# Decode block with cached attention: keys turned by VectorE block transposes, column-tiled row matmuls, and one ring for the whole load stream

## The chip, the cores and the metric

The kernel runs on one core of a Trainium2 chip. The metric is the device time of one execution in microseconds (us); where several runs exist, their median is quoted.

The time of a run is about 2 us longer than the span in its profile, which goes from the first to the last instruction (before: 455.95 against 453.9). Positions inside the profile are counted from the start of the span.

## The reference

One decode step for a batch of 8: an adaLN block around grouped-query attention with a cache, then an adaLN block around a gated MLP. Everything is bf16.

```python
# x [8,1,1024], c [8,1024], w_mod [1024,6144], wq [1024,4096], wo [4096,1024]
# k_cache, v_cache [8,4,8192,128]   (32 query heads share 4 key/value heads)
# W_gate, W_up [1024,3584], W_down [3584,1024]
mod = silu(c) @ w_mod            # six rows: sa, ca, ga, sb, cb, gb
h = layernorm(x) * (1 + ca) + sa
q = h @ wq                       # [8,32,128]
p = softmax(q @ k^T / sqrt(128)) # over 8192 keys
x = x + ga * ((p @ v) @ wo)
h = layernorm(x) * (1 + cb) + sb
x = x + gb * ((relu(h @ W_gate) * (h @ W_up)) @ W_down)
```

The caches are 134 MB and the weights 51 MB; every byte is used once. A "head" below is one pair of batch and key/value head: 32 of them, each with 2 MB of K and 2 MB of V.

## The kernel before

The kernel is written engine by engine. SP issues the weight and K loads, ACT issues the V loads. Weights have four slots of 2 MB, K has four, V three; each load waits for the last reader of its slot.

```python
NW = 4
NV = 3
NKT = 4
# ... (cut)
def issue_k(eng, n):
    b, p = n // G, n % G
    slot = n % NKT
    if n - NKT >= 0:
        eng.wait("pe", ("sdone", n - NKT))
    eng.dma(T.ksl[:, slot, :], A_k_cache[b, p].rearrange("(k c) d -> k (c d)", k=128), "k%d" % slot)

def issue_v(eng, n):                       # called on ACT's queue
    # ... (cut)
    if n - NV >= 0:
        eng.wait("pe", ("pvdone", n - NV))
    eng.dma(T.vsl[:, slot, :], A_v_cache[b, p].rearrange("(k c) d -> k (c d)", k=128), "v%d" % slot)
```

Scores and the value product both take a block of the cache as the stationary operand (of a matmul's two operands the one that a weight load brings in first; the other is called the moving one), so that each head needs 64 matmuls of eight columns for each. Softmax is done once for a whole batch element (four heads), with the keys in the partitions.

```python
# scores of one head: 64 matmuls, K block stationary
for cix in range(NCX):
    pe.op(lambda e, ...: e.matmul(
        T.S_ps[:, col:col + REP], kv[:, cix, :], T.qT[:, b, REP * p:REP * (p + 1)], start=True, stop=True), ...)
# ... (cut)
# the order on PE
for b in range(B):
    st_phase(b)
    if b >= 1:
        pv_pairs(b - 1, [0, 1])
    softmax_pe_1(b)
    if b >= 1:
        pv_pairs(b - 1, [2, 3])
    softmax_pe_2(b)
```

All projections take the weights as stationary blocks of 128 x 128 with an eight-column moving operand. W_down is loaded in rows of 2 KB, W_gate and W_up in rows of 7 KB:

```python
wblocks.append(("gu", kc, [(lambda r: r[:, 0:F], B_W_gate[128 * kc:128 * (kc + 1), :]),
                           (lambda r: r[:, 4096:4096 + F], B_W_up[128 * kc:128 * (kc + 1), :])]))
# ... (cut)
B_W_down[r0:r0 + rr, :].rearrange("(kk p) n -> p kk n", p=128)
# ... (cut: after the last W_down matmul)
dve.op(... tT <- tT * gb); dve.op(... outT_b <- tT + x1T)
# eight transposes on PE, one copy on DVE, one store on SP
```

Of the kernel before, what the change touches and what calls it, by code (L numbers as in the profile page):

```python
# [11 lines left out]
class _Eng:  # L12

    def __init__(self, K, name):
        self.K = K
        self.name = name
        self.count = 0
        self.e = None
        self.sem = None
        self.muted = True  # L20

    def _live(self):
        return self.K.emit and not self.muted

    def op(self, fn, key=None, sync=True):
        if sync:
            self.count += 1
        if self._live():
            ins = fn(self.e)
            if sync:  # L30
                ins.then_inc(self.sem, 1)
        if key is not None:
            self.mark(key)
        return self.count

    def mark(self, key):
        k = (self.name, key)
        if self.K.emit:
            assert self.K.ev[k] == self.count, (k, self.K.ev[k], self.count)
        else:  # L40
            assert k not in self.K.ev, k
            self.K.ev[k] = self.count

    def wait(self, eng_name, key):
        if self._live():
            val = self.K.ev[(eng_name, key)]
            self.e.wait_ge(self.K.engs[eng_name].sem, val)

    def wait_self(self):
        if self._live() and self.count > 0:  # L50
            self.e.wait_ge(self.sem, self.count)

    def wait_dma(self, sem_name, value):
        if self._live():
            self.e.wait_ge(self.K.dsem[sem_name], value)

    def dma(self, out_ap, in_ap, sem_name):
        c = self.K.dcnt.get(sem_name, 0) + 16
        self.K.dcnt[sem_name] = c
        if self._live():  # L60
            self.e.dma_start(out_ap, in_ap).then_inc(self.K.dsem[sem_name], 16)  # L61
        return c


class _K:
    pass


class _T:
    pass  # L70


DBG = {}


def bass_adaLN_cond__gqa_block_cached__glu_gated_reglu__decode_kernel(
    nc: bass.Bass,
    A_x: bass.AP,
    A_k_cache: bass.AP,
    A_v_cache: bass.AP,  # L80
    A_wq: bass.AP,
    A_wo: bass.AP,
    B_x: bass.AP,
    B_W_gate: bass.AP,
    B_W_up: bass.AP,
    B_W_down: bass.AP,
    c: bass.AP,
    w_mod: bass.AP,
    out: bass.AP,
):  # L90
    B, _, D = A_x.shape
    _, G, Sk, Dh = A_k_cache.shape
    HQD = A_wq.shape[1]
    Hq = HQD // Dh
    REP = Hq // G
    F = B_W_gate.shape[1]
    assert B == 8 and D == 1024 and Dh == 128 and Hq == 32 and G == 4 and REP == 8
    assert F % 128 == 0 and w_mod.shape[1] == 6 * D
    assert Sk % 128 == 0
    NCX = Sk // 128  # L100
    NCOL = NCX * G * REP
    assert NCOL <= 2048
    KC = D // 128
    NKC2 = F // 128
    inv_sqrt_dh = float(Dh) ** -0.5
    EPS = 1e-5
    NW = 4
    NV = 3
    NKT = 4

    K = _K()
    K.ev = {}
    K.emit = False
    K.dcnt = {}
    K.pe_rank = None
    K.engs = {nm: _Eng(K, nm) for nm in ("sp", "act", "pool", "dve", "pe")}

    wblocks = []
    for kc in range(KC):
        wblocks.append(("mod", kc, [(lambda r: r[:, 0:6 * D], w_mod[128 * kc:128 * (kc + 1), :])]))  # L120
    for jb in range(KC // 2):
        wblocks.append(("wq", jb, [(lambda r: r[:, 0:2 * HQD].rearrange("p (k n) -> p k n", n=HQD),
                                    A_wq[256 * jb:256 * (jb + 1), :].rearrange("(kc p) n -> p kc n", p=128))]))
    for blk in range(4):
        wblocks.append(("wo", blk, [(lambda r: r[:, 0:KC * 1024].rearrange("p (k n) -> p k n", n=1024),
                                     A_wo[1024 * blk:1024 * (blk + 1), :].rearrange("(hh d) n -> d hh n", d=128))]))
    for kc in range(KC):
        wblocks.append(("gu", kc, [(lambda r: r[:, 0:F], B_W_gate[128 * kc:128 * (kc + 1), :]),
                                   (lambda r: r[:, 4096:4096 + F], B_W_up[128 * kc:128 * (kc + 1), :])]))
    wd_rows = []  # L130
    r0 = 0
    while r0 < F:
        rr = min(1024, F - r0)
        wd_rows.append((r0, rr))
        r0 += rr
    for di, (r0, rr) in enumerate(wd_rows):
        wblocks.append(("wd", di, [(lambda r, rr=rr: r[:, 0:(rr // 128) * 1024].rearrange("p (k n) -> p k n", n=1024),
                                    B_W_down[r0:r0 + rr, :].rearrange("(kk p) n -> p kk n", p=128))]))
    assert F <= 4096 and 6 * D <= 8192
    widx = {(w[0], w[1]): i for i, w in enumerate(wblocks)}  # L140
    n_phaseA = widx[("wo", 0)]

    last_k_user = {}
    for n in range(B * G):
        last_k_user[n % NKT] = n
    last_v_user = {}
    for n in range(B * G):
        last_v_user[n % NV] = n
    big_regions = Sk >= KC * 1024
    regionsC = [("w", j) for j in range(NW)]  # L150
    if big_regions:
        regionsC += [("k", j) for j in range(NKT)] + [("v", j) for j in range(NV)] + [("s", 0)]
    blocksC = list(range(n_phaseA, len(wblocks)))
    load_order = list(blocksC)
    wplan = {}
    _cnt = {}
    region_last = {}
    for i in range(n_phaseA):
        region = ("w", i % NW)
        free = ("pe", ("wdone", region_last[region])) if region in region_last else None  # L160
        semname = "w%d" % (i % NW)
        _cnt[semname] = _cnt.get(semname, 0) + 16 * len(wblocks[i][2])
        wplan[i] = (region, free, semname, _cnt[semname])
        region_last[region] = i
    holder_t = {}
    for r in regionsC:
        holder_t[r] = region_last[r] if r in region_last else (n_phaseA - 0.5)
    assign = {}
    for i in load_order:
        r = min(regionsC, key=lambda rr_: (holder_t[rr_], regionsC.index(rr_)))  # L170
        assign[i] = r
        holder_t[r] = i
    _wj = [0]
    for i in load_order:
        region = assign[i]
        if region in region_last and region_last[region] >= n_phaseA:
            free = ("pe", ("wdone", region_last[region]))
        elif region[0] == "w":
            free = ("pe", ("sdone", min(B * G - 1, (2 + _wj[0]) * G + G - 1)))
            _wj[0] += 1  # L180
        elif region[0] == "k":
            free = ("pe", ("pvdone", (B - 2) * G + G - 1))
        elif region[0] == "v":
            free = ("pe", ("pvdone", last_v_user[region[1]]))
        else:
            free = ("pe", ("pvdone", B * G - 1))
        semname = {"w": "w%d", "k": "ck%d", "v": "cv%d", "s": "cs%d"}[region[0]] % region[1]
        _cnt[semname] = _cnt.get(semname, 0) + 16 * len(wblocks[i][2])
        wplan[i] = (region, free, semname, _cnt[semname])
        region_last[region] = i  # L190

    T = _T()

    def run():
        K.dcnt = {}
        for e in K.engs.values():
            e.count = 0
        sp, act, pool, dve, pe = (K.engs[n] for n in ("sp", "act", "pool", "dve", "pe"))

        def wregion(i):  # L200
            region = wplan[i][0]
            if region[0] == "s":
                return T.scr[:, 0:8192]
            base = {"w": T.wslot, "k": T.ksl, "v": T.vsl}[region[0]]
            return base[:, region[1], 0:8192]

        def load_wblock(eng, i):
            kind, idx, pieces = wblocks[i]
            region, free, semname, val = wplan[i]
            if free is not None:  # L210
                eng.wait(free[0], free[1])
            r = wregion(i)
            v = None
            for dst_fn, src in pieces:
                v = eng.dma(dst_fn(r), src, semname)
            assert v == val, (i, v, val)

        def pe_wait_wblock(i):
            pe.wait_dma(wplan[i][2], wplan[i][3])

        PB = [T.X_ps, T.OT_ps]

        def issue_k(eng, n):
            b, p = n // G, n % G
            slot = n % NKT
            if n - NKT >= 0:
                eng.wait("pe", ("sdone", n - NKT))
            eng.dma(T.ksl[:, slot, :], A_k_cache[b, p].rearrange("(k c) d -> k (c d)", k=128), "k%d" % slot)

        def issue_v(eng, n):  # L230
            b, p = n // G, n % G
            slot = n % NV
            if n - NV >= 0:
                eng.wait("pe", ("pvdone", n - NV))
# [537 lines left out]
```

## Time and profile before

| | before |
|---|---|
| time, median of 3 runs | 455.95 us (455.82 to 457.14) |
| span of the profile | 453.9 us |
| moved by DMA | 186.40 MB, mean 411 GB/s |
| busy: PE, DVE | 40%, 22% |
| mean granted TensorE clock | 0.96 of full speed |

The first lines to look at are those of the page's 40 slices: the mean busy share of the 16 DMA engines, in tenths, and what they moved.

```profile
DMA  7999999999999999999999999999999989999992
GB/s 309 431 431 426 422 435 428 429 430 372 427 429 424 435 422 425 422 433 422 430 423 430 431 416 430 430 428 419 436 424 432 394 357 428 420 423 424 414 405 77
```

DMA is at 9 (90% or more) in nearly every slice. PE and DVE have room. This kernel is bound by its loads, and a gain has to show in this row. The next view of the page lists the DMA queues: packets, bytes, and the share of the time of 16 engines that they took.

```profile
q1 hardware_dynamic: 17008, 118.54, 62.5%
q10 hardware_dynamic: 4608, 67.11, 34.8%
q8 instruction: 45, 0.74, 0.6%
```

q1 carries SP's loads, q10 ACT's. q8 carries instructions that PE fetches: 45 packets of 16 KB. They take 0.6% of the engines' time.

The third view is a table of windows. The columns are the window, its width, busy time of PE, weight loads, DVE, ACT and POOL with the number of instructions, the granted clock, the DMA share and GB/s.

```profile
core 0: us, PE busy (x) PEld busy (x) DVE busy (x) ACT busy (x) POOL busy (x), PEclk, DMA share, GB/s
0.00:12.00 12.00, 2.36 (x78) 2.25 (x79) 5.87 (x12) 3.79 (x4) 1.28 (x9) 1.00 0.81 317
44.00:52.00 8.00, 3.18 (x104) 3.00 (x104) 1.71 (x6) 0.00 (x0) 0.00 (x0) 1.00 1.00 422
100.00:118.00 18.00, 12.10 (x390) 11.24 (x390) 5.44 (x4) 0.00 (x0) 0.00 (x0) 1.00 0.96 392
350.00:370.00 20.00, 12.26 (x390) 11.43 (x390) 2.99 (x4) 0.00 (x0) 0.00 (x0) 1.00 0.90 369
440.00:454.00 14.00, 7.45 (x232) 6.93 (x232) 2.47 (x9) 0.00 (x0) 0.00 (x0) 0.50 0.36 136
```

The full rate is about 428 GB/s: 425 to 430 in long undisturbed stretches. With that as the yardstick (an estimate), a window's lost time is its width times (1 - rate / 428). That is 3.1 us at the start, 1.5 us in the dip near 110 us, 2.8 us in the dip near 360 us and 9.5 us at the end.

The start and the end can be read closer. The first lines are from the timeline (start, duration, engine, line, operation, count); the second set is the end of the chain of work that ended last.

```profile
0.74 0.39 SPq L61 DMA_DIRECT2D stage_b<-in_c_dram  x1
1.51 8.36 SPq L61 DMA_DIRECT2D wslot<-in_w_mod_dram  x5
8.09 1.42 PE L569 MATMUL X_ps<-siluT,wslot 128*128 128x8 bf16 x48 [2.63 <-DMA wslot<-in_w_mod_dram]
```

```profile
447.29 1.34 PE X_ps L651 x45
448.63 0.87 PE OT_ps L651 x32
450.32 1.03 PE PT_ps L660 x8
451.37 0.68 DVE stage_b L482
```

The first weight load is issued at 1.51 us, behind two small loads. The last piece of W_down is used from 447.29 us, and 6.6 us pass from there to the end. The groups of instructions give the price of one instruction (busy us, mean ns, then the idle time before them with what ended it):

```profile
L525 PE MATMUL OT_ps<-scr,vsl 128*128 128x8 bf16 x2048 | 60.1, 168 | 87.5 <-DMA vsl<-in_A_v_cache_dram 76.7
L508 PE MATMUL S_ps<-qT,ksl 128*128 128x8 bf16 x2048 | 58.3, 168 | 89.5 <-DMA ksl<-in_A_k_cache_dram 76.5
L427 DVE TENSOR_REDUCE guacc<-scr 128x32 f32<-128x2048 bf16 x8 | 28.5, 3568 | 15.8 <-ACT scr L324 15.8
```

### The profile page before, as it was taken

To read this page: it belongs to the slowest core of one execution; us is meant where nothing else is said; L and a number is where in the kernel's file an instruction comes from. 1 tells how busy PE (TensorE), PEld (TensorE's weight loads), DVE (VectorE), ACT (ScalarE), POOL (GpSimd) and SP (SyncE) were. 2 spreads that over 40 slices of the span, in tenths; PEclk is the share of its full clock that TensorE was granted. 3 is DMA by queue.
4 is the path that set the end of the run, shared out by engine and by line. 5 is a ranking of instruction groups with operands and counts; after the bars stand their busy time and mean duration, and the time that the engine had idled before them with its cause. 6 is when DMAs were issued, how large, how long until landed. Compare 5 with 4: busy or idle time off the path is not lost.

```text
span 453.9 us, 11940 instructions
## 1 busy us (share of the span) xinstructions
PE 183.6 (40%) x5784; PEld 170.6 (38%) x5784; DVE 100.9 (22%) x120; ACT 22.5 (5%) x16; POOL 1.3 (0%) x9
## 2 busy tenths in 40 slices
PE   1212433418445226072407240733073573364655
PEld 1212433307345226062406240633063462263655
DVE  5000200062322320043004300430043043003321
ACT  3000001010100100001000100100010011000000
POOL 1000000000000000000000000000000000000000
PEclk9999999999999999999999999999999999999555
DMA  7999999999999999999999999999999989999992
GB/s 309 431 431 426 422 435 428 429 430 372 427 429 424 435 422 425 422 433 422 430 423 430 431 416 430 430 428 419 436 424 432 394 357 428 420 423 424 414 405 77
DMA packets 21662, 186.40 MB, mean 411 GB/s; under 512 B 1624, under 2 KB 1624, under 8 KB 11376
## 3 DMA queue, kind: packets, MB, share of 16 engines
q1 hardware_dynamic: 17008, 118.54, 62.5%
q10 hardware_dynamic: 4608, 67.11, 34.8%
q8 instruction: 45, 0.74, 0.6%
q14 instruction: 1, 0.01, 0.0%
HBM read 185.63 MB, written 0.02 MB: 409 GB/s over the span
## 4 chain that ended last, share of the span: by engine, by line
DMA 65%; PE 19%; DVE 6%; issue 5%; another core or an unknown queue 3%; ACT 1%; SPq 1%
DMA ksl<-in_A_k_cache_dram 43%; DMA vsl<-in_A_v_cache_dram 12%; DMA wslot<-in_w_mod_dram 10%; PE S_ps L508 7%; PE OT_ps L525 4%; PE X_ps L612 2%; DVE guacc L427 2%; PE X_ps L634 1%; PE OT_ps L634 1%; DVE scr L422 1%; PE X_ps L651 1%; ACT scr L324 1%; PE S_ps L494 1%; SPq L61 1%
## 5 line engine op out<-in xcount | busy, mean ns | idle before, releaser
L525 PE MATMUL OT_ps<-scr,vsl 128*128 128x8 bf16 x2048 | 60.1, 168 | 87.5 <-DMA vsl<-in_A_v_cache_dram 76.7
L508 PE MATMUL S_ps<-qT,ksl 128*128 128x8 bf16 x2048 | 58.3, 168 | 89.5 <-DMA ksl<-in_A_k_cache_dram 76.5
L525 PEld LDWEIGHTS OT_ps<-scr,vsl 128*128 128x128 bf16 x2048 | 57.3, 104 | 89.8 <-DMA vsl<-in_A_v_cache_dram 77.8
L508 PEld LDWEIGHTS S_ps<-qT,ksl 128*128 128x128 bf16 x2048 | 56.5, 104 | 91.2 <-DMA ksl<-in_A_k_cache_dram 74.1
L410 DVE TENSOR_REDUCE guacc<-S_ps 128x32 f32<-128x2048 f32 x8 | 18.3, 2292 | 145.5 <-PE S_ps L508 145.5
L427 DVE TENSOR_REDUCE guacc<-scr 128x32 f32<-128x2048 bf16 x8 | 28.5, 3568 | 15.8 <-ACT scr L324 15.8
L324 ACT ACTIVATE scr<-scr 128x2048 bf16<-128x2048 f32 x8 | 15.3, 1909 | 286.4 <-DVE scr L422 286.4
L422 DVE TENSOR_TENSOR scr<-S_ps,guacc 128x2048 f32<-128x2048 f32 x8 | 18.3, 2291 | 0.3
L569 PE MATMUL X_ps<-siluT,wslot 128*128 128x8 bf16 x192 | 5.8, 168 | 17.4 <-DMA wslot<-in_w_mod_dram 17.4
L569 PE MATMUL OT_ps<-siluT,wslot 128*128 128x8 bf16 x192 | 5.8, 168 | 16.5 <-DMA wslot<-in_w_mod_dram 16.5
L569 PEld LDWEIGHTS X_ps<-siluT,wslot 128*128 128x128 bf16 x192 | 5.4, 104 | 17.7 <-DMA wslot<-in_w_mod_dram 15.0
L569 PEld LDWEIGHTS OT_ps<-siluT,wslot 128*128 128x128 bf16 x192 | 5.4, 104 | 16.8 <-DMA wslot<-in_w_mod_dram 16.8
L430 DVE RECIPROCAL guacc<-X_ps 1x32 f32<-1x32 f32 x8 | 2.8, 346 | 37.5 <-PE X_ps L542 37.5
L612 PE MATMUL X_ps<-ot_sb,wslot 128*128 128x8 bf16 x256 | 7.3, 168 | 4.2 <-issue 3.5
L612 PEld LDWEIGHTS X_ps<-ot_sb,wslot 128*128 128x128 bf16 x256 | 7.1, 104 | 4.4 <-issue 3.6
L413 DVE TENSOR_REDUCE guacc<-X_ps 32x1 f32<-32x128 f32 x8 | 2.2, 278 | 22.9 <-PE X_ps L534 22.9
L537 PEld LDWEIGHTS X_ps<-guacc,ones 32*128 32x128 f32 x16 | 4.0, 306 | 8.7 <-DVE guacc L415 8.7
L537 PE MATMUL X_ps<-guacc,ones 32*128 32x32 f32 x16 | 5.0, 406 | 5.1 <-DVE guacc L415 5.1
L386 DVE TENSOR_TENSOR modT<-OT_ps,modT 128x384 f32<-128x384 f32 x4 | 2.2, 558 | 19.5 <-PE OT_ps L569 19.5
L545 PE MATMUL X_ps<-guacc,ones 1*128 1x32 f32 x16 | 5.0, 406 | 3.5 <-DVE guacc L430 3.5
L587 PE MATMUL X_ps<-hT,wslot 128*128 128x8 bf16 x128 | 3.7, 168 | 6.2 <-DMA wslot<-in_A_wq_dram 6.2
L587 PE MATMUL OT_ps<-hT,wslot 128*128 128x8 bf16 x128 | 3.7, 168 | 6.0 <-DMA wslot<-in_A_wq_dram 6.0
(88 smaller groups left out, 107.3 us busy)
## 6 DMA issues: line engine op xcount, KB each, us to landing
vsl<-in_A_v_cache_dram ACTq DMA_DIRECT2D x32, 2048.0 KB, 18.7
ksl<-in_A_k_cache_dram SPq DMA_DIRECT2D x32, 2048.0 KB, 29.4
wslot<-in_w_mod_dram SPq DMA_DIRECT2D x8, 1536.0 KB, 22.5
wslot<-in_A_wq_dram SPq DMA_DIRECT2D x4, 2048.0 KB, 17.0
wslot<-in_A_wo_dram SPq DMA_DIRECT2D x4, 2048.0 KB, 38.5
wslot<-in_B_W_down_dram SPq DMA_DIRECT2D x3, 2048.0 KB, 20.3
ksl<-in_B_W_gate_dram SPq DMA_DIRECT2D x4, 896.0 KB, 23.8
ksl<-in_B_W_up_dram SPq DMA_DIRECT2D x4, 896.0 KB, 25.5
```

The lines of the kernel that those rows point to most:

```text
L324: act.op(lambda e: e.activation(T.pt[:, b % 2, 0:NCOL], T.ssub[:, 0:NCOL], ACT.Exp), key=("exp", b))
L410: dve.op(lambda e: e.tensor_reduce(T.mpart[:, :], T.S_ps[:, 0:NCOL].rearrange("p (c j) -> p j c", c=NCX), AX.X, ALU.max), key=("mpart", b))
L422: dve.op(lambda e: e.tensor_tensor(out=T.ssub[:, 0:NCOL].rearrange("p (c j) -> p c j", c=NCX), in0=T.S_ps[:, 0:NCOL].rearrange("p (c j) -> ...
L427: dve.op(lambda e, b=b: e.tensor_reduce(T.lpart[:, :], T.pt[:, b % 2, 0:NCOL].rearrange("p (c j) -> p j c", c=NCX), AX.X, ALU.add), key=(" ...
L508: pe.op(lambda e, b=b, p=p, kv=kv, cix=cix, col=col: e.matmul(T.S_ps[:, col:col + REP], kv[:, cix, :], T.qT[:, b, REP * p:REP * (p + 1)], ...
L525: pe.op(lambda e, p=p, cix=cix, col=col, vv=vv, ptv=ptv: e.matmul(T.OT_ps[:, col:col + REP], vv[:, cix, :], ptv[:, cix, REP * p:REP * (p + ...
L537: pe.op(lambda e: e.matmul(T.X_ps[:, 128:160], T.ones[0:32, 0:128], T.diag[0:32, 0:32], start=True, stop=True), key=("P2", b))
L545: pe.op(lambda e: e.matmul(T.X_ps[:, 192:224], T.ones[0:1, 0:128], T.rrow[0:1, 0:32], start=True, stop=True), key=("P4", b))
L569: pe.op(lambda e, fb=fb, pb=pb, reg=reg, kc=kc: e.matmul(pb[:, fb * B:fb * B + B], reg[:, 128 * fb:128 * (fb + 1)], T.siluT[:, kc, :], sta ...
L587: pe.op(lambda e, hq=hq, kk=kk, pb=pb, reg3=reg3, jb=jb: e.matmul(pb[:, hq * B:hq * B + B], reg3[:, kk, 128 * hq:128 * (hq + 1)], T.hT[:, ...
L612: pe.op(lambda e, fb=fb, hq=hq, wvs=wvs: e.matmul(T.X_ps[:, fb * B:fb * B + B], wvs[hq // 8][:, hq % 8, 128 * fb:128 * (fb + 1)], T.ot_sb[ ...
L634: pe.op(lambda e, fb=fb, pb=pb, reg=reg, kc=kc, cbase=cbase, wbase=wbase: e.matmul(pb[:, cbase + fb * B:cbase + fb * B + B], reg[:, wbase ...
```

## The change

The intent is to keep PE and DVE further from the limit per byte loaded, and above all to let the loads run without ever waiting for a batch-wide softmax. The kernel is a rewrite. Its parts are:

- **One ring for all loads.** Nine slots of 2 MB hold modulation weights, wq, K, V, wo, gate, up and down in the order of use; all are issued on SP's queue, each as soon as its place has been read.
- **K turned in SBUF.** Four DVE transposes of 32-bit words per head (in blocks of 32 x 32, as the kernel's indexing takes them) bring the head dimension into the partitions. Scores then take the query as the stationary operand and 512 keys as the moving one, 16 matmuls per head, with the query padded with zeros so that all 16 accumulate into one bank. Softmax becomes a short sequence per head.
- **Column-tiled row matmuls.** In modulation, wq, wo and W_down the activations are stationary (32 columns), and four matmuls of 256 or 512 columns write four different groups of 32 output partitions.
- **Longer rows.** W_gate, W_up and W_down are read in 14 KB runs per partition. For gate and up this leaves the columns of a stationary block 14 bytes apart.
- **A dependency tracker.** Every operation names what it reads and writes, and waits are derived from that.

The core of the diff:

```diff
-    NW = 4
-    NV = 3
-    NKT = 4
+    SLOT = 8192
+    NSLOT = 9
 ... (cut)
+        def pump():
+            while stream:
+                key, src, n = stream[0]
+                lo = cursor[0] if cursor[0] + n <= NSLOT * SLOT else 0
+                if P.unread("arena", lo, lo + n):
+                    return
+                ... (cut)
+                P.op("sp", lambda e, dst=dst, src=src: e.dma_start(dst, src), writes=[slot_r(lo, lo + n)], dma=True)
+        wm_src = w_mod.rearrange("(p k) n -> p (k n)", k=KC)
+        g_src = B_W_gate.rearrange("(p k) n -> p (k n)", k=KC)
+        d_src = B_W_down.rearrange("(q p r) n -> q p (r n)", p=128, r=FR)
 ... (cut)
+        P.op("pool", lambda e: e.memset(c_r[:], 0.0), writes=[R("c_r")])
+        P.op("pool", lambda e: e.memset(x_r[:], 0.0), writes=[R("x_r")])
+        for t, src, nm in ((c_r, c2, "c_r"), (x_r, x2, "x_r")):
+            for j in range(4):
+                P.op("act", lambda e, t=t, src=src, j=j: e.dma_start(t[32 * j:32 * j + B, :], src[:, 256 * j:256 * (j + 1)]),
+                     writes=[("%s" % nm, 0, 1)], dma=True)
 ... (cut)
-                pe.op(lambda e, ...: e.matmul(T.S_ps[:, col:col + REP], kv[:, cix, :], T.qT[:, b, REP * p:REP * (p + 1)], ...))
+            P.op("dve", lambda e: e.transpose(ktb[:, to:to + QE].bitcast(dt.uint32), arena[:, lo:lo + QE].bitcast(dt.uint32)), ...)
+            fns.append(lambda e, t=t, r=r: e.matmul(
+                ps[:, n % 2, :].rearrange("p (c k) -> p c k", k=32), qpad[:, n % NQ, t * 2 + r, 24 - 8 * i:152 - 8 * i],
+                kv[:, :, t, :, r], start=(i == 0 and t == 0 and r == 0), stop=(i == 3 and t == 1 and r == 1)))
 ... (cut)
+                for j in range(4):
+                    fns.append(lambda e, ...: e.matmul(
+                        ps[32 * j:32 * j + 32, 1, 0:256], hmT[:, f, :], w[:, r, j, :], start=(f == 0), stop=(f == KF - 1),
+                        tile_position=(0, 32 * j)))
```

The product with V keeps its form, 64 matmuls of eight columns per head.

## The prediction

> **What bounds the kernel now.** The page's slices show the DMA row at 9 (90% or more) almost everywhere, moving 186.4 MB at a mean 411 GB/s. A table of windows gives 429 to 430 GB/s while weights stream (12 to 36 us), 427 in attention (200 to 350 us), both at DMA share 1.00. PE is busy 40%, DVE 22%: neither limits. The whole load at 428 GB/s would take 435 us (estimate from those rates); the span is 453.9 us. So only about 19 us can be won, and what happens on PE or DVE counts only if it starves the loads. Where the 19 us lie:
> - start: 0 to 12 us moves 317 GB/s; the first weight load is issued at 1.51 us, behind two small loads. About 3 us lost.
> - two dips, slice 10 (372 GB/s) and 350 to 375 us (381 GB/s), where load queues wait for the per-batch softmax: 1.5 + 2.8 us.
> - the end, 420 to 443 us, at 407 to 413 GB/s with many small packets (W_down comes in 2 KB rows): about 2 us.
> - the last loads finish raggedly (443 to 447 us), then 6.6 us of matmuls, transposes, copy and output: about 9 us.
>
> **What the change does.**
> - QK: 64 matmuls of 8 columns per head (1.8 us) become 16 of 512 columns, about 3.5 us at full clock (estimate). PV stays (64 in 1.9 us). PE per head about 5.8 us.
> - DVE gains four 1024-word transposes per head. [...] The trace's 2048-element ops take 2.29 us, so about 1.15 us each; with probability transpose, row max and small ops 6.4 us per head (estimate).
> - One head's K and V are 4.19 MB, 9.8 us at 428 GB/s. PE 5.8 and DVE 6.4 both fit: attention stays load-bound.
> - Batch softmax (2.3 + 2.3 + 3.6 us on DVE, 1.9 on ACT, eight times) becomes a per-head pipeline; with nine 2 MB slots in one ring both dips should go: -4.3 us.
> - First weight load first on its queue: -0.7 us. Longer rows in gate, up, down: -1.5 to -2 us. About 40% fewer PE instructions to fetch: -0.5 us.
> - [...] one ring by itself brings no bandwidth. The trace agrees: 430 with one queue, 427 with two.
> - Tail: 28 column-tiled matmuls after the last load, perhaps 3.6 us, two 0.4 us DVE ops and the output, about 6.5 us: no gain.
>
> Sum: about -7.5 to -8 us of 455.95: 448.0 us, 80% range 443.5 to 455. Faster by over 2%: 0.36; within 2%: 0.58; slower: 0.06.
>
> **What would show it.** DMA at 9 in all slices, no dip below 420 GB/s before the tail; DVE busy 45 to 50%, about 1.15 us a transpose; the chain mostly DMA; the load queue waiting for free slots, never DVE for long.
>
> **What would make it wrong.** Four-byte transposes at half rate would cost 2.2 us each, some 11 us of DVE per head against 9.8: about 35 us slower. Gate and up weights are now read with a 14-byte stride: if a weight load takes 100 ns instead of 27, gate and up need 45 us of PE against 34 us of loads, and the tail grows by up to 7 us. PE at half clock in attention (9.4 us per head) would leave no slack. Conversely, concurrent column tiles would shorten the tail by 2 us and make it over 2% faster.

The sum came to 7.5 to 8 us less than 455.95; the terms as listed (4.3, 0.7, 1.5 to 2, 0.5) add up to 7.0 to 7.5. Its 1.15 us for a transpose is an estimate, half of the 2.29 us that a 2048-element operation took in the profile before. Its 3.5 us for the score matmuls of a head and its 3.6 us for the last 28 matmuls are estimates; the changed kernel shows 16 x 217 ns = 3.5 us at a granted clock of 1.00, and 1.71 us at 0.50.

## The result, and the profile after

The changed kernel takes **455.47 us** (median of 4 runs, 455.42 to 455.54). The outputs are right. The kernel before, run beside it, took 456.54 us (4 runs, 455.82 to 457.41). The ratio is 0.9981, with a 95% interval from 0.9964 to 0.9998: the same within 2%. Ratios here are the mean time of one kernel's fast runs over that of the other's of the same rounds, so not quite the ratio of the medians that are quoted. The predicted 448.0 us was 7.5 us too low, and the time lies just above the range.

The same lines of the page, now of the changed kernel:

```profile
DMA  8999699999999999999999999999999999999992
GB/s 347 436 420 425 267 428 433 424 429 426 425 429 423 429 425 432 423 429 427 427 425 426 428 426 426 429 423 428 425 432 423 429 406 387 404 429 426 424 420 91
```

```profile
q1 hardware_dynamic: 16288, 185.61, 97.2%
q8 instruction: 27, 0.44, 0.4%
```

```profile
core 0: us, PE busy (x) PEld busy (x) DVE busy (x) ACT busy (x) POOL busy (x), PEclk, DMA share, GB/s
0.00:12.00 12.00, 0.00 (x0) 0.00 (x0) 0.00 (x0) 0.00 (x0) 4.83 (x13) 1.00 0.88 359
44.00:52.00 8.00, 6.64 (x76) 3.28 (x80) 1.52 (x5) 0.20 (x1) 0.00 (x0) 1.00 0.53 197
100.00:118.00 18.00, 14.00 (x163) 7.63 (x162) 12.33 (x18) 0.99 (x3) 1.64 (x8) 0.78 1.01 427
350.00:370.00 20.00, 15.89 (x169) 8.25 (x167) 12.76 (x19) 1.56 (x4) 0.82 (x4) 0.82 1.00 423
370.00:390.00 20.00, 13.13 (x234) 8.83 (x238) 10.49 (x18) 2.84 (x5) 0.00 (x0) 0.78 1.04 385
440.00:454.00 14.00, 5.05 (x84) 2.81 (x84) 0.85 (x2) 0.00 (x0) 0.00 (x0) 0.50 0.33 137
```

Both dips of before are gone: 427 GB/s where there were 392, and 423 where there were 369. But slice 5 of the GB/s row has a new hole, 267, and the window from 44 to 52 us shows it at 197 GB/s. The table adds up the lost time, worked out as above (the sums are of unrounded values); the last column is the first experiment below.

| window, us | lost before | lost after | lost with the chain of small loads cut |
|---|---|---|---|
| 0 to 12 | 3.1 | 1.9 | 1.9 |
| 44 to 52 | 0.1 | 4.3 | 0.0 |
| 100 to 118 | 1.5 | 0.0 | 0.2 |
| 350 to 370 | 2.8 | 0.2 | 0.6 |
| 370 to 390 | 0.1 | 2.0 | 1.6 |
| 390 to 440 | 1.2 | 0.4 | 1.3 |
| 440 to the end | 9.5 | 9.1 | 8.3 |
| sum | 18.2 | 18.0 | 13.8 |

The loss at 370 to 390 us is of another kind. W_o is loaded there in rows of 2 KB, and with the loads alone (experiment 3) this window also moves only 398 GB/s. (In the trace of the changed kernel a row of 2 KB takes 88 ns and one of 16 KB 613 ns, so 16 KB take 704 ns in short rows.) It is no wait for compute.

The groups show that the compute side is as predicted:

```profile
L404 DVE STREAM_TRANSPOSE kt<-arena 128x1024 uint32<-128x1024 uint32 x128 | 153.3, 1218 | 114.6 <-DMA arena<-in_A_k_cache_dram 114.6
L413 PE MATMUL ps<-kt,qpad 128*128 128x512 bf16 x512 | 165.3, 491 | 2.0 <-POOL qpad L393 2.0
L453 PE MATMUL ps<-pT,arena 128*128 128x8 bf16 x2048 | 56.1, 166 | 48.4 <-DVE pT L443 48.4
L521 PE MATMUL ps<-hT,arena 128*128 128x8 bf16 x448 | 24.8, 194 | 9.3 <-DMA arena<-in_B_W_gate_dram 3.7
```

A transpose of 1024 words takes 1218 ns (predicted 1150), and the page has DVE busy 48% (predicted 45 to 50%). The start, from the timeline:

```profile
0.74 1.92 SPq L225 DMA_DIRECT2D arena<-in_w_mod_dram  x4
1.08 17.02 ACTq L260 DMA_DIRECT2D c_r<-in_c_dram  x4
2.70 46.79 SPq L225 DMA_DIRECT2D arena<-in_A_wq_dram  x4
18.14 19.59 ACTq L260 DMA_DIRECT2D x_r<-in_A_x_dram  x4
37.76 1.28 ACT L271 ACT_TABLE_LOAD   x1 [37.76 <-DMA x_r<-in_A_x_dram]
46.37 3.93 PE L327 MATMUL ps<-arena,hT 128*32 128x512 bf16 x36
```

This is the story of the hole. The eight small loads of c and x, 4 KB each, are issued one after another from 1.08 to 37.4 us: within each group of four, each waits for the landing of the one before. ACT's first operation starts only at 37.76 us, PE's first weight matmul at 46.37 us. By then the ring is full: four 3 MB loads and three of wq fill its nine slots (18.9 MB, 44 us at 428 GB/s), and the fourth load of wq cannot be issued before the first modulation weights have been read. It is the last of the four in the line that starts at 2.70 us and lasts 46.79 us.

Each small load lands 5.0 to 7.1 us after its issue. A load of 128 rows, shared evenly, is 8 rows for each of the 16 engines; a 24 KB row takes 0.93 us in this trace, so one such share lasts 7.4 us, an estimate. A wait behind about one share of a large load would agree in size; how an engine chooses between the queues is not shown.

The end of the chain:

```profile
412.04 36.49 DMA arena<-in_B_W_down_dram
448.57 1.71 PE ps L537 x28
450.31 0.43 DVE lu L541
450.76 0.42 DVE ob L543
```

The tail after the last landing is shorter than before, 5.0 us instead of 6.6, but it starts 1.3 us later.

One more reading was needed, of events that no summary shows. The completion semaphore of every large load goes up sixteen times: the trace has 16 events for each of the 88. They are read here as the moments at which the 16 DMA engines finished their parts, though not which engine it was. The rows in the trace bear this out: while the stream is full about 16 are in flight, and at the end of the changed kernel, where 7 of the 16 events lie between 442.35 and 443.10 us and the rest from 445.38 to 448.52, 16 rows are in flight at 441.5 us, 9 from 443 to 444.5, 3 at 447 and none at 448.2. For the last load of W_down (the spread is the time from the first of the sixteen to the last):

| kernel | PE instruction packets (q8) | first engine done, us | last engine done, us | spread, us |
|---|---|---|---|---|
| before | 45 | 443.79 | 447.26 | 3.5 |
| after | 27 | 442.35 | 448.52 | 6.2 |

In the changed kernel this spread grows in steps: 0.5 to 0.7 us until about 47 us, 1.7 at 57, 3.2 at 191, 4.8 at 320, 6.2 at 418. The steps of 1.2 to 1.6 us are somewhat longer than the 1.07 us that one instruction packet takes; experiment 8 comes back to this. So some engines fall behind for good, and the last load is complete only when the most lagging one has done its part.

### The profile page after: what moved, and what is told of

It is laid out like the page before. It is cut to its first block, busy times and chain, and to the rows that moved or that the text cites. A ratio compares the mean times of both kernels' runs of the same rounds, so it can differ in the third digit from the quotient of the medians.

```text
span 453.6 us, 7815 instructions
## 1 busy us (share of the span) xinstructions
PE 291.1 (64%) x3514; PEld 167.4 (37%) x3514; DVE 217.6 (48%) x333; ACT 33.2 (7%) x78; POOL 31.0 (7%) x141
## 4 chain that ended last, share of the span: by engine, by line
DMA 80%; PE 10%; DVE 8%; issue 1%; ACT 0%; ACTq 0%; POOL 0%; DVEq 0%; POOLq 0%
DMA arena<-in_A_k_cache_dram 60%; DMA arena<-in_B_W_down_dram 8%; DMA arena<-in_A_wo_dram 4%; DMA x_r<-in_A_x_dram 4%; DMA c_r<-in_c_dram 4%; PE ps L453 4%; DVE kt L404 3%; PE ps L521 2%; PE ps L327 2%; DVE pT L443 1%; PE ps L350 1%; DVE hT L279 0%; DVE lu L274 0%; PE ps L537 0%; PE ps L413 0%
## 5 line engine op out<-in xcount | busy, mean ns | idle before, releaser
L404 DVE STREAM_TRANSPOSE kt<-arena 128x1024 uint32<-128x1024 uint32 x128 | 153.3, 1218 | 114.6 <-DMA arena<-in_A_k_cache_dram 114.6
L413 PE MATMUL ps<-kt,qpad 128*128 128x512 bf16 x512 | 165.3, 491 | 2.0 <-POOL qpad L393 2.0
L413 PEld LDWEIGHTS ps<-kt,qpad 128*128 128x128 bf16 x512 | 61.9, 121 | 94.9 <-issue 66.2
L453 PE MATMUL ps<-pT,arena 128*128 128x8 bf16 x2048 | 56.1, 166 | 48.4 <-DVE pT L443 48.4
L453 PEld LDWEIGHTS ps<-pT,arena 128*128 128x128 bf16 x2048 | 54.2, 96 | 62.8 <-issue 62.5
L393 POOL COPY qpad<-qR 32x32 bf16<-32x32 bf16 x128 | 26.2, 205 | 320.6 <-PE ps L413 257.0
L437 ACT ACTIVATE prb<-ps,bias 128x512 bf16<-128x512 f32 x32 | 22.0, 687 | 285.0 <-DVE mjt L431 285.0
L521 PE MATMUL ps<-hT,arena 128*128 128x8 bf16 x448 | 24.8, 194 | 9.3 <-DMA arena<-in_B_W_gate_dram 3.7
L521 PEld LDWEIGHTS ps<-hT,arena 128*128 128x128 bf16 x448 | 24.4, 153 | 9.7 <-DMA arena<-in_B_W_gate_dram 3.9
L423 PEld LDWEIGHTS ps<-identf,negm 128*128 128x128 f32 x64 | 13.1, 256 | 37.7 <-DVE negm L419 37.7
L443 DVE STREAM_TRANSPOSE pT<-prb 128x512 bf16<-128x512 bf16 x32 | 21.5, 672 | 1.7 <-ACT prb L437 1.7
```

What stands on the lines that cost most here:

```text
L393: P.op("pool", lambda e, n=n, Q=Q: e.tensor_copy(qpad[32 * Q:32 * Q + 32, n % NQ, :, 24 + 32 * Q:32 + 32 * Q], qR[32 * Q:32 * Q + 32, :, n ...
L404: P.op("dve", lambda e: e.transpose(ktb[:, to:to + QE].bitcast(dt.uint32), arena[:, lo:lo + QE].bitcast(dt.uint32)), reads=[slot_r(lo, lo ...
L413: fns.append(lambda e, t=t, r=r: e.matmul(ps[:, n % 2, :].rearrange("p (c k) -> p c k", k=32), qpad[:, n % NQ, t * 2 + r, 24 - 8 * i:152 - ...
L423: P.op("pe", lambda e: e.matmul(ps[:, 2, 0:128], negm[:, n % 2:n % 2 + 1].to_broadcast([128, 128]), identf[:], start=True, stop=True), rea ...
L437: P.op("act", lambda e: e.activation(prb[:, z, :], ps[:, z, :], ACT.Exp, bias=bias[:, z:z + 1], scale=scale, accum_out=lall[:, n:n + 1]), ...
L443: P.op("dve", lambda e: e.transpose(pT[:, z, :], prb[:, z, :]), reads=[R("prb", z, z + 1)], writes=[R("pT", z, z + 1)])
```

## The experiments

Two reasons came out of this comparison. One: the small loads form a false chain, which lets the ring fill and costs the time of the hole. Two: the gain from the vanished dips is not lost at one place but at the end, because some DMA engines lag, and PE's instruction packets may be what makes them lag. The rivals were that the hole is only idle time that other waits would show anyway, that the raggedness comes from the shape or the number of the loads, and that the tail's matmuls are to blame. The quoted expectations use letters for these theories.

Kernels of one call ran on the same chip: the first four together, the next four, then four more, then the last one. Where two kernels of different calls are compared, the ratios to the kernel before are given too.

### 1. The small loads without the false chain

Each of the four loads of c writes its own rows, but all declare the whole tile as written, and so does the zeroing before them. The tracker therefore makes each wait for the landing of the one before. The experiment declares what each really writes. The loads still wait for the zeroing.

```diff
-        P.op("pool", lambda e: e.memset(c_r[:], 0.0), writes=[R("c_r")])
-        P.op("pool", lambda e: e.memset(x_r[:], 0.0), writes=[R("x_r")])
+        P.op("pool", lambda e: e.memset(c_r[:], 0.0), writes=[R("c_r_z")])
+        P.op("pool", lambda e: e.memset(x_r[:], 0.0), writes=[R("x_r_z")])
 ...
-                     writes=[("%s" % nm, 0, 1)], dma=True)
+                     reads=[R(nm + "_z")], writes=[R(nm, j, j + 1)], dma=True)
 ... (readers of c_r and x_r: R("c_r", 0, 4), R("x_r", 0, 4))
```

> The eight small loads of c and x are declared disjoint, so that none waits for the landing of the one before it; nothing else changes. Theory A (the stall of 44 to 52 us comes from that chain of false waits, each of which takes about 6 us because the small load lands behind megabytes that are already queued): all eight are issued by about 4 us and have landed by about 7 us, the first PE work starts before 15 us instead of at 44 us, the dip of slice 5 (267 GB/s) is gone, and the time falls by about 4 us to 451.3. Theory B (the second queue is itself held back while the first one is full, whatever the waits): the small loads still land one by one until about 37 us and the time stays at 455.4.

Measured: **451.49 us** (451.27 to 451.70), ratio to before 0.9889 (0.9860 to 0.9918). Three lines of its timeline, and one of its table of windows:

```profile
1.07 1.73 ACTq L260 DMA_DIRECT2D c_r<-in_c_dram  x4
2.84 1.40 ACTq L260 DMA_DIRECT2D x_r<-in_A_x_dram  x4
21.40 1.90 PE L327 MATMUL ps<-arena,hT 128*32 128x512 bf16 x16
```

```profile
44.00:52.00 8.00, 3.80 (x32) 0.92 (x32) 0.00 (x0) 0.00 (x0) 0.00 (x0) 0.50 1.00 426
```

All eight loads are issued by 4.3 us, PE's first weight matmul starts 25 us earlier, and the hole is gone (426 GB/s). The time falls by 4.0 us, which is the area of the hole, 4.3 us, almost whole: just before the hole the engines were within 0.7 us of one another, so all of them stood idle together. The false chain is shown. PE starts at 21.4 us, later than expected, which does no harm: the loads that are already issued last until about 44 us.

All later experiments on the changed kernel start from this version, called the **unchained kernel** here: 451.49 us, last load done at 444.51 us, spread 6.5 us.

### 2. The small loads first on the same queue

The eight small loads go to SP's queue, ahead of the weights.

```diff
-                P.op("act", lambda e, t=t, src=src, j=j: e.dma_start(t[32 * j:32 * j + B, :], src[:, 256 * j:256 * (j + 1)]),
+                P.op("sp", lambda e, t=t, src=src, j=j: e.dma_start(t[32 * j:32 * j + B, :], src[:, 256 * j:256 * (j + 1)]),
 ... (the ring's first loads are issued after these)
```

> As the run without the chain, but the eight small loads go out first, on the same queue as the weights. Both theories: they land within about 2 us of their issue, as in the kernel before, and PE starts by about 12 us. The price is that the first weight load is issued about 2.4 us later (eight issues of 0.28 us). So no dip at 44 us, about 2.4 us lost at the start, 453.5 us in all: some 2 us slower than the run without the chain under theory A, some 2 us faster than the changed kernel under theory B.

Measured: 454.18 us (453.89 to 454.34), ratio 0.9947, 2.7 us more than the unchained kernel and 0.7 us over the expectation. The first weight load is issued at 3.85 us instead of 0.74, and nothing fills the gap: 255 GB/s in the first 12 us instead of 362. Here eight small issues in front of the stream delay its first load by 3.1 us and cost 2.7 us of time. On ACT's queue, free of the false chain, they did not delay it.

### 3. The loads alone (wrong result)

All compute is removed, and nothing waits for compute: a load waits only for the landing of the load that held its slot before. The stream of loads and the final stores remain. The result is wrong; this is a measurement of the loads.

```diff
-                if P.unread("arena", lo, lo + n):
-                    return
 ... (all compute and the small loads removed)
```

> Wrong result on purpose (zeros): the same 75 large loads through the same nine-slot ring in the same order, each waiting only for the landing of the load that held its slot, and no compute at all. It measures the load stream by itself. Theory C (the ragged end, 6.2 us between the first and the last of the 16 completions of the last load, comes from instruction fetches of PE that share some of the DMA engines): with no PE instructions to fetch the completions of the last load lie within 1 us and the time is about 442.5. Theory D (some engines are slower by themselves, or the deep ring lets them drift): the spread still grows to 5 us or more and the time is about 447.

Measured: 443.79 us (443.74 to 444.14), against an expected 442.5. (The 75 loads of the expectation are a slip; there are 88.) The last load has its first engine done at 437.96 us, as in the unchained kernel (438.06), but its last at 438.82 us: a spread of 0.9 us instead of 6.5. So the loads themselves, their order, size and rows, do not make the end ragged. Something that runs beside them does. This kernel has no q8 packets.

### 4. More PE instructions

Thirty-two dummy matmuls of eight columns are added per head. PE has room for them (busy 72% with them); what they add besides shows in q8.

```diff
+            P.op("pe", [lambda e: e.matmul(ps[0:32, 6, 0:8], identb[:, 0:32], identb[:, 0:8], start=True, stop=True)] * 32,
+                 reads=[R("identb")], writes=[bank(6)])
```

> As the run without the chain, plus 32 tiny matmuls per head into a spare bank, 2048 more PE instructions in all (131 KB, about 8 more fetches of 16 KB on top of 27). PE has the time: 7 of 9.8 us per head are busy now. Theory C: the spread of the last load's completions grows from about 6 us by 1.4 us for one or two more fetches on the engines that lag, and the time is 1 to 3 us above the run without the chain. Theory D: the same time within 0.4 us and the same spread.

Measured: 453.00 us (452.56 to 453.45), 1.5 us more than the unchained kernel. Its line of q8:

```profile
q8 instruction: 35, 0.57, 0.5%
```

Eight packets more, and the spread grows from 6.5 to 7.6 us, while the first engine is done at 438.10 us as before.

### 5. Short rows again

W_down is read in 2 KB rows again, and the stationary columns of gate and up are taken next to each other.

```diff
-        d_src = B_W_down.rearrange("(q p r) n -> q p (r n)", p=128, r=FR)
+        d_src = B_W_down.rearrange("(q r p) n -> q p r n", p=128, r=FR)
 ...
-                    w = arena[:, base + (kk % 2) * F:...].rearrange("p (q x r) -> p q r x", q=NB, r=FR)
+                    w = arena[:, base + (kk % 2) * F:...].rearrange("p (q r x) -> p q r x", q=NB, r=FR)
```

> The run without the chain, with the row order of W_down as before (each partition takes 2 KB rows, 128 rows apart, instead of 14 KB in one piece), and so gate and up columns contiguous instead of 14 bytes apart. Packets of 2 KB took 88 ns and packets of 14 KB 539 ns (seven of 2 KB: 616 ns), so 7.3 MB over 16 engines should take 2.4 us longer: about 453.9 if the rows matter by that much; 452.4 if only by the 407 to 429 GB/s that the windows of the kernel before and of the changed one show; 451.5 if the gain of long rows was nothing. The weight loads of gate and up should fall back from 56 ns to 27 ns a matmul, off the critical path: no effect on the time.

Measured: 452.94 us (452.92 to 453.93). Its neighbours on the same chip that equal the unchained kernel took 451.57 and 451.56 us (6 and 7 below), so the long rows of W_down are worth 1.4 us. The prediction's 1.5 to 2 included gate and up, whose rows stay long here. Gate and up fall from 24.8 to 13.1 us of PE for 448 matmuls, from 55 ns to 29 ns each, both at a granted clock of 0.50:

```profile
L521 PE MATMUL ps<-hT,arena 128*128 128x8 bf16 x448 | 13.1, 168 | 18.8 <-DMA arena<-in_B_W_gate_dram 8.5 <-DMA arena<-in_B_W_up_dram 7.9 <-DVE hT L279 2.4
```

So a stationary block whose columns lie 14 bytes apart costs 26 ns more per matmul here; the runs do not show by what mechanism. It is not on the chain of loads, so it costs no time here.

### 6. Six slots instead of nine

```diff
-    NSLOT = 9
+    NSLOT = 6
```

> The run without the chain with 6 slots in the ring instead of 9. Theory E (the load stream is bound by the slowest of 16 engines, and the depth of the ring only has to cover the use of a slot): the same time within 0.7 us (451.5) and the same spread of completions at the end, about 6 us. Theory F (depth itself lets the engines drift apart and so costs time at the end): the spread shrinks to about 3 us and the time falls by 2 us or more. If six slots are too few for the life of a V slot (about 12 us beside 4.9 us a load), dips appear in attention and it is 5 us or more slower.

Measured: 451.57 us (451.49 to 452.71), the same as with nine (ratios 0.9883 and 0.9889). Three slots less change nothing, so the depth of the ring is not what the time hangs on. The spread was 4.6 us instead of 6.5 (about 6 had been expected), but with first and last engine at 440.02 and 444.63: the leading engines wait more, the last one ends as before. This was the first hint that only the lagging engine counts.

### 7. The order of the column tiles in the tail

All seven matmuls of one group of output partitions are issued before the next group, so that neighbouring matmuls write the same partitions.

```diff
-            for r in range(FR):
-                for j in range(4):
+            for j in range(4):
+                for r in range(FR):
```

> The run without the chain, with the two inner loops of the W_down matmuls exchanged: seven matmuls in a row go to one column tile, then the next tile, so that neighbours no longer sit in different tiles. Theory G (28 matmuls take 1.69 us at half clock because four tiles work at once): now up to 28 x 213 ns = 6 us per block, more than the 4.3 us between loads, so PE falls behind and the time grows by 4 to 10 us, to 455.5 or more. Theory H (the tiles bring nothing, the matmuls are that fast anyway): the same 451.5.

Measured: 451.56 us (451.31 to 453.44): the same. The last block of 28 matmuls takes 1.98 us instead of 1.71. The expected size was missed. (Its 213 ns a matmul is an estimate, half of the 427 ns between score matmuls of 512 columns at a clock of 0.50; number 11 measures 213.) But the granted clock in this block was 1.00 here and 0.50 in the unchained kernel, so at the same clock the new order would be the slower one (two earlier blocks of this run took 3.54 us each, those of the unchained kernel 1.68 to 1.69), and this run alone does not settle whether the tiles overlap. Number 11 does.

### 8. Fewer PE instructions

The product with V is turned: the probabilities are stationary and V moves, 16 column-tiled matmuls of 512 columns, one copy on ACT and four summing matmuls, in place of 64 matmuls.

```diff
-            for cc in range(NC):
-                fns.append(lambda e, cc=cc: e.matmul(ps[:, 3, col:col + J], vv[:, cc, :], pv_[:, cc % 16, cc // 16, :],
-                                                     start=(cc == 0), stop=(cc == NC - 1)))
+            for cc in range(16):
+                g = cc % 4
+                fns.append(lambda e, cc=cc, g=g: e.matmul(ps[32 * g:32 * g + 32, 5 + z, :], pT[:, z, 32 * cc:32 * cc + 32], vv[:, cc],
+                                                          start=(cc < 4), stop=(cc >= 12), tile_position=(0, 32 * g)))
+            P.op("act", lambda e: e.activation(xs[:, z, :], ps[:, 5 + z, :], ACT.Copy), ...)
 ... (then four matmuls sum the four groups)
```

> The run without the chain, with PV turned as well: 16 column-tiled matmuls of 512 columns (the probabilities of four chunks stationary, V moving), a copy by ACT and four summing matmuls, instead of 64 pairs of weight load and matmul per head. PE instructions fall from about 7030 to 4210, fetches of 16 KB from 27 to about 16. Theory C (fetches make some DMA engines lag): the spread of the last load's completions falls from 6.4 us to about 4 us and the time by 1.5 to 2.5 us, to about 449.5. Theory D: spread and time as without this, 451.5.

Measured: **448.57 us** (448.57 to 448.63), ratio 0.9811 (0.9788 to 0.9834). That is 3.0 us less than its neighbours 6 and 7 on the same chip.

```profile
q8 instruction: 16, 0.26, 0.2%
```

Eleven packets fewer, and the spread falls to 3.7 us; the first engine is done at 438.08 us, as in all of these. Put together, first the kernels with an untouched load stream:

| kernel | q8 packets | first engine done, us | last engine done, us | time, us |
|---|---|---|---|---|
| 3, loads alone | 0 | 437.96 | 438.82 | 443.79 |
| 8, fewer PE instructions | 16 | 438.08 | 441.75 | 448.57 |
| 1, unchained | 27 | 438.06 | 444.51 | 451.49 |
| 4, more PE instructions | 35 | 438.10 | 445.68 | 453.00 |

The leading engines do not care; the last one ends (445.68 - 438.82) / 35 = 0.20 us later for every packet. Between 8 and 4 the time rises by (453.00 - 448.57) / 19 = 0.23 us per packet. (q14 carries six more instruction packets, of 8 KB, in 8, 1 and 4 alike.)

A packet's record lasts 1.07 us, but it holds up its engine for longer. How far the sixteen completions of the last load lie behind the first adds up to 4.1, 34.6, 48.4 and 61.1 us in the four kernels of the table. Between 8 and 4 that is (61.1 - 34.6) / 19 = 1.4 us per packet. One case in the trace of 8: a packet runs from 211.46 to 212.48 us, no row starts on one of the engines meanwhile, and that engine's next row takes 1.16 us instead of 0.61, so it loses 1.55 us. The trace of the changed kernel shows the same: during its q8 packets 15.1 rows are in flight in the mean, 16.1 otherwise, and at the end of each of the 20 packets up to 357 us one row starts that takes 1.08 to 1.16 us. Shared evenly among 16 engines, 1.4 us would be 0.09 us. The cost is more than twice the even share: the packets fall unevenly. In 8, 1 and 4 alike, seven engines end within 1.3 us of the first, and nine end at least 2.9 us after it. The engine that is furthest behind sets the end.

The number of packets follows the number of PE instructions: matmuls plus weight loads divided by 256 give 45.2, 27.5, 35.5 and 16.5 for before, unchained, 4 and 8, and q8 has 45, 27, 35 and 16 packets. So in these four kernels there is one packet of 16 KB to about 256 PE instructions, and in the kernels of the table, which keep all 16 engines full, each costs 0.2 us.

### 9. The last load split

On top of 8, the last load of W_down is split into six rows and one, so that most of the last matmuls can run before the last landing.

```diff
-            load(("wd", i), d_src[i], FR * D)
+            if i < NB - 1:
+                load(("wd", i), d_src[i], FR * D)
+            else:
+                load(("wd", i), d_src[i][:, 0:6 * D], 6 * D)
+                load(("wd", i, "b"), d_src[i][:, 6 * D:7 * D], D)
```

> The run with fewer PE instructions, and the last W_down load split into six rows and one row (12 KB and 2 KB a partition), so that only 4 of its 28 matmuls wait for the last byte. After the last landing 0.3 us of matmuls instead of 1.7 us: 1.2 to 1.4 us less, about 447.3 us; more than 2% faster than the kernel before.

Measured: 447.94 us (5 runs, 447.79 to 448.32), ratio 0.9802 (0.9785 to 0.9820). Against 8 this is 0.6 us by the medians and 0.4 us by the ratios, whose intervals overlap; 1.2 had been expected. The last 28 matmuls still run as one block from 441.06 us, 1.71 us long, because the two parts land only 0.6 us apart: both wait for the lagging engine. It is the best version, about 2.0% faster than the kernel before, and the interval around 0.98 leaves it open whether it is above or below 2%.

### 10. The lead of the fast engines taken away

The load of K for head 28 waits until the nine loads before it have landed on all engines. That gives every engine the same start again, at the price of a pause.

```diff
+                o = P.op("sp", lambda e, dst=dst, src=src: e.dma_start(dst, src), writes=[slot_r(lo, lo + n)], dma=True)
+                if key == ("k", 28):
+                    P.ops[o]["deps"] |= {(d, "raw") for d in issued[-NSLOT:]}
+                issued.append(o)
```

> The run without the chain, with one added wait: the load of K number 28 is issued only when all loads before it have landed. That makes one full dip of the load queue late in attention, when the first and the last engine are about 4.9 us apart; attention has loads and time in hand. Theory I (a dip costs its area, as the prediction counted the dips of the kernel before): the leading engines stand idle for 4.9 + 1.6 us, all of them for 1.6 us, on average some 4 us, and the time grows by 4 us or more, to 455.5. Theory J (the time is that of the engine that lags most, and a dip only lets the others wait for it): the time grows by 1.5 to 2 us (landing, semaphore, issue, first byte) to about 453.3, and the completions of the last load lie within 2.5 us instead of 6.4.

Measured: 455.42 us (455.12 to 455.72), ratio 0.9965, 3.9 us more than the unchained kernel by the medians, 3.5 by the ratios. The window around the pause:

```profile
322.00:336.00 14.00, 11.22 (x97) 5.42 (x95) 6.32 (x11) 1.56 (x4) 0.81 (x4) 0.82 0.67 262
```

The area of this dip is 14 x (1 - 262/428) = 5.4 us. The leading engines end 6.9 us later than in the unchained kernel (444.99 against 438.06), the last one 3.7 us later (448.23 against 444.51). (The 1.5 to 2 us of theory J are an estimate. In the trace of the changed kernel 0.41 us pass from the end of the last row, 448.11, to the last event, and 1.04 us from the first issue, 0.74, to the first row: 1.45 us together.) So the dip's area is again not what it costs, but by itself this run could not separate the price of the pause from the price of restarting the stream. Number 13 does.

### 11. The tail without column tiles

All four parts of the W_down matmuls write the same group of output partitions, and four copies put them where they belong.

```diff
-                        ps[32 * j:32 * j + 32, 1, 0:256], hmT[:, f, :], w[:, r, j, :], start=(f == 0), stop=(f == KF - 1),
-                        tile_position=(0, 32 * j)))
+                        ps[0:32, 1 + j // 2, 256 * (j % 2):256 * (j % 2) + 256], hmT[:, f, :], w[:, r, j, :],
+                        start=(f == 0 and j % 2 == 0), stop=(f == KF - 1), skip_group_check=True, tile_position=(0, 0)))
+        for j in range(4):
+            P.op("dve", lambda e, j=j: e.tensor_copy(lt[32 * j:32 * j + 32, :], ps[0:32, ...]), ...)
```

> The run without the chain, with all W_down matmuls in one column tile (the first 32 PSUM partitions, two banks), and four small copies by DVE (about 0.3 us each) to bring the result to its places. Theory G (the 60 ns a matmul come from four tiles working at once): at half clock 256 columns take 213 ns, a block 6 us, more than the 4.3 us between loads: 460 us or more; at full clock 3 us a block, about 454. Theory H (the column tiles bring nothing): only the copies, 452.5 to 452.8.

Measured: 454.99 us (454.57 to 455.88), ratio 0.9958, 3.5 us more by the medians, 3.1 by the ratios. From its chain, and then from that of the unchained kernel:

```profile
444.51 3.25 PE ps L537 x28
```

```profile
444.55 1.72 PE ps L537 x28
```

The same 28 matmuls take 3.25 us here and 1.72 in the unchained kernel, 115 against 60 ns each. The four copies add 1.8 us, and the sum of both is nearly the whole difference. The granted clock makes the case stronger: it was 1.00 in this block and only 0.50 in that of the unchained kernel. Where this run has a clock of 0.50, in an earlier block, its matmuls of this line start 213 ns apart. So matmuls in different column tiles overlap here (60 against 213 ns at the same clock), and between these two runs this shortens the tail by 1.5 us.

### 12. More PE instructions in the kernel before

The same dummy matmuls as in 4, in the kernel before.

```diff
+                for _ in range(32):
+                    pe.op(lambda e: e.matmul(T.D_ps[0:32, 0:8], T.identb[:, 0:32], T.identb[:, 0:8], start=True, stop=True),
+                          sync=False)
```

> The kernel before, with 32 tiny matmuls into a spare bank after each head's PV: 2048 more PE instructions, 8 more fetches of 16 KB on top of 45, the same addition that cost 1.5 us in the changed kernel without the chain. Theory J (also the kernel before ends with its most lagging engine): 1 to 2 us slower. Theory K (its two dips are slack in which the lagging engines catch up): within 0.5 us of the kernel before.

Measured: 458.67 us (458.28 to 459.28) against 456.92 us for the kernel before on the same chip, ratio 1.0037 (1.0018 to 1.0056): 1.75 us more, for eight packets more.

```profile
q8 instruction: 53, 0.87, 0.7%
360.00:370.00 10.00, 6.63 (x230) 6.37 (x227) 2.29 (x1) 0.00 (x0) 0.00 (x0) 1.00 0.67 256
```

That is 0.22 us per packet, the same price. But it is paid elsewhere. The spread at the end is unchanged, 3.4 us. It is the second dip that got deeper: 256 GB/s from 360 to 370 us, where the kernel before has 311. Just before it, in the kernel before, the sixteen completions of one load of K lie up to 12 us apart, and those of the loads of V that land after 370 us at most 3.3 us; here those of K lie up to 15 us apart. So the second dip of the kernel before is at least in part the leading engines waiting for the lagging ones. So not all of its area was time that a deeper ring alone could win.

### 13. The same pause with the loads alone (wrong result)

The edit of 10 in the kernel of 3. There no engine lags, so the pause costs only the restart.

> Wrong result on purpose (zeros): the loads alone (443.8 us) with the same full drain before K number 28. Here the engines stay within 1 us of one another, so the drain costs the restart of the queue and nothing else. In the kernel with compute the same drain cost 3.9 us, with the engines 4.9 us apart. Theory J (the idle time of engines that are ahead is free; only what the last engine loses counts): the drain costs nearly as much here, 3 to 3.9 us, 447 to 447.7 us in all. Theory I (idle time costs its area, averaged over the engines): of the 3.9 us some 2.5 us were the lead of the engines ahead, so here it costs 1.3 to 1.6 us, about 445.2.

Measured: 446.87 us (446.58 to 447.02), 3.1 us more than 3 by the medians, 2.5 by the ratios. The spread at the end was 0.7 us. So of the 3.9 us in number 10 about 3.1 (by the ratios 2.5 of 3.5) are the restart of the queue, and 0.8 (1.0 by the ratios) are left for having taken away the lead of the engines in front, which was about 5 us at most and 2.7 us in the mean of the sixteen. Idle time of the leading engines is mostly free.

## Why the prediction was wrong

The prediction's own numbers imply when it thought the last load would land: 448.0 us of time, less 2.0 us between time and span, less its tail of 6.5 us, is 439.5 us. The measured sum then closes:

| term | us |
|---|---|
| predicted time | 448.0 |
| last landing of the unchained kernel, 444.51 instead of 439.5 | +5.0 |
| its tail from there to the end of the span, 5.1 instead of 6.5 | -1.4 |
| its time less its span, 1.9 instead of 2.0 | -0.1 |
| false chain of the small loads (experiment 1) | +4.0 |
| sum | 455.5 |
| measured | 455.47 |

Point by point:

- **What bounds the kernel: right.** Loads bound both kernels, and PE and DVE fit. The rate in attention is 427 GB/s with two queues and 427 with one (100 to 118 us after), so one ring neither gained nor lost bandwidth here. The score matmuls start 217 ns apart where the granted clock is 1.00, so 3.5 us per head, as the prediction had estimated; at 0.50 they start 427 ns apart.
- **The transposes: right.** 1218 ns against 1150 predicted. That is 1.19 ns for each of the 1024 four-byte elements; a transpose of 512 two-byte elements takes 672 ns, 1.31 ns for each. So the four-byte transposes did not run at half rate, which the prediction had named as a danger.
- **Longer rows: right.** 1.4 us for W_down alone (experiment 5), predicted 1.5 to 2 with gate and up. The danger of the 14-byte stride was seen rightly in kind: 55 ns per matmul instead of 29, not the feared 100, and off the chain.
- **The start: right in sign.** 1.2 us less lost in the first 12 us, predicted 0.7.
- **The failed step: "with nine 2 MB slots in one ring both dips should go: -4.3 us".** Both dips went, and the 4.3 us did not come. From the kernel before to the unchained one the last landing moved from 447.26 to 444.51 us, by 2.75 us. The rows (1.4) and the start (1.2) account for nearly all of it. The dips and the fetches together, put at 4.3 + 0.5 us, brought about 0.1 us net. (This is what is left by subtraction; no run takes away the dips alone.) The reason shown by 8, 10, 12 and 13 is that a dip's area is the mean idle time of 16 engines, while the time is set by the engine that is furthest behind. The leading engines' idle time is mostly free, and it comes back at the end as a wider spread, 6.5 us instead of 3.5.
- **A cost not seen: the new hole.** The prediction said that no dip below 420 GB/s would come before the tail. It read the small loads as small. Their false chain, visible in the diff as one tile name written eight times in two groups, delayed the first compute to 46 us; the nine slots lasted only until 44 us. This cost 4.0 us, shown by experiment 1. Nor did the prediction see that W_o's short rows would keep 370 to 390 us at 385 GB/s.
- **A term mis-sized: "About 40% fewer PE instructions to fetch: -0.5 us".** The number of packets fell from 45 to 27 as predicted. The price was taken from their mean share of the engines; measured, each costs about 0.2 us of the time (4, 8, and 12 in the kernel before). What the 18 fewer packets brought against the kernel before cannot be separated from the dips.
- **The tail: "no gain" was wrong in the small.** After the last landing 6.6 us became 5.0, because the column tiles overlap (11). This "2 us" chance was named in the prediction as the upside; it came, and the later landing took it back.

What stays open: that the instruction packets fall on some engines more than on others is read from completions and from the gaps in the rows. Which engines these are, and why, is not recorded. How much of the first dip of the kernel before, and which exact share of the second, was waiting for lagging engines is not settled. Why the granted clock's mean is lower in the changed kernel (0.78 with PE busy 64%, against 0.96 with 40%) was not tested, as PE does not bound it.

## What to carry to other kernels

When loads bound a kernel, count the time of the DMA engine that ends last, not the mean idle share: read the sixteen completions of a load beside the GB/s row before putting a price on a dip. Here a packet of PE's instructions held up one of those DMA engines by about 1.4 us, so fewer and larger matmuls can be worth microseconds even where PE is not the limit (3.0 us in experiment 8; 0.2 us per 256 instructions). And in a program whose waits are derived from declared reads and writes, look first at the small loads at its head: a write declared too wide makes a chain of landings, here 5.0 to 7.1 us each, and it can stop the whole stream (4.0 us in experiment 1).
